# An SSM block with its gradients on one core: base powers fetched at other ticks, products with C moved, some work handed to ScalarE

## The chip, the core and the metric

One Trainium2 chip, one core of it, one launch. The metric is the device time of one execution in microseconds (us), lower is better. The engines of the core work from queues of their own, each in the order in which the program lists its instructions: PE (matrix products and transposes), VectorE (DVE), ScalarE (ACT), GpSimd (POOL), and SP, which here issues nearly all DMAs. They wait for each other through semaphores.

## The reference, cut to what matters

```python
def _A_ref(u, A_re, A_im, B_re, B_im, C_re, C_im, log_dt, Dskip):
    dt = jnp.exp(log_dt)[:, None]
    logdA = dt * (A_re + 1j * A_im)
    dB = dt * (B_re + 1j * B_im)
    P = jnp.exp(logdA[:, :, None] * l[None, None, :])         # l = 0 .. 2047
    K = jnp.einsum("dn,dnl,dn->dl", Cc, P, dB).real
    ...                                                        # y = irfft(rfft(u) * rfft(K)), the causal convolution
    return y + u * Dskip
x = A_u
xn = _layernorm(x)
s = _A_ref(xn, ...)
g = silu(einsum("bsf,fd->bsd", silu(einsum("bsd,df->bsf", xn, w1)), w2))
out = x + s * g
```

The result is `out` and the gradients of all its inputs for a given `grad_out`. L = 2048 rows, D = 512 channels, N = 128 states, F = 1792; all tensors are bf16.

## The kernel before, in words

Five stages follow each other. Stage 1 (to about 205 us of the profile) holds nearly all of the change. It does four things at once:

- `Setup`: loads x in four groups of four row tiles, takes mean and variance of each tile (`stats(i)`), normalizes it (`norm(i)`: `nb` = -mean * rstd, then `xn`), and brings the parameters A, B, C into the layout needed (`param(i)`: PE transposes into `pt_par`, a copy to `pa_...`). `lam` is eight ScalarE exponentials.
- `gen_ffn_fwd`: the forward feed-forward. Its 28 blocks (four groups of rows with seven pairs of column tiles each) give on PE a `ps_h`, from which ScalarE makes `aT` (silu) and `hs` (a copy that is stored to `hTd`). PE transposes `aT` into `pt_a`, VectorE copies that into `ak`, which is stored to `akd`. One row group later `gen_o` makes `ps_o` from `aT`; ScalarE makes `g2` (silu) and `o2` from it, which are stored to `gd` and `od`, and VectorE multiplies `g2` with `grad_out`, loaded into `G2`. "Block k" or aT(k) below counts the 28 blocks from 0.
- `dft_table_phases`: tables of sines and cosines: `tb_r`, `tb_v` on VectorE, `tb_w`, `tb_f` on ScalarE, `ps_m` and `pt_ti` on PE, stored to `TFd` and `TId`. Its first instruction is GpSimd's iota `kv`, from which VectorE casts `kf`. Its pool is opened where the pool of `Setup` (with `x_sb`) has been closed.
- `power_phases`: the base powers of exp(dt A), in eleven pairs of exponents. For pair i: `X` multiplies magnitudes on GpSimd (`ex`), `A` takes fractions of angles on VectorE (`b_r`, `b_f`), `B` takes sines on ScalarE (`b_w`, `b_s`), `C` multiplies both on VectorE into the result buffer `XYg` (two buffers), `S` stores it to `XYd` in DRAM. `setup0` makes the angle per step (`tau`), `setup1` the product of C with dt B (`Ctr`, `nCti`, twice 128x512) and the block `one`, which takes a buffer of the tag of `XYg` too. Pairs 5 and 6 (exponents 32 to 128) use `Ctr` and `nCti`.

The order is written out by hand: `stage_1` first runs six blocks with `Setup` beside them, then counts a tick n from 6 on, one block (or later half a tile of `gen_o`) per tick; what a tick starts is listed by `put`. Copies and stores handed to `later` are emitted at the end of the tick.

```python
    put(6, s0); put(8, s1); put(9, pS, "one")
    for i in range(len(PAIRS)):
        x = 7 + 2 * i + i // 5
        put(x - 1, pX, i); put(x, pA, i); put(x + 1, pB, i); put(x + 2, pC, i); put(x + 3, pS, i)
```

So the last pair (1024 and 2048) is stored at tick 32 and the one before it (768 and 896) at tick 29. At tick 30 the base powers of the first quarter of the channels are read back from `XYd` into `XYc`, in three slices, which lies in a buffer of `aT`. From tick 33 on, `copy_tables` spreads `XYc` into `X`, `Y` and `CY` on ScalarE, and `chunk_tables` multiplies out the remaining powers on VectorE (`m`). The two entries of the last pair come as a fourth fetch, `XYl`, in stage 2, where the first Fourier products (`ps_f`, `XU`) run as well. `Dskip` is loaded in `Setup` into `Dsk` and added to row 0 of the convolution kernel `K_b` at the end of stage 2.

A DMA that SP is to issue waits in SP's queue for what it needs, and with it all that stands behind it.

Of the kernel before, what the change touches and what calls it, by code (L numbers as in the profile page):

```python
# [14 lines left out]
P = 128  # L15
# [252 lines left out]
class Setup:  # L268


    def __init__(self, k, W1, W2, pr, p1):
        nc, const = k.nc, k.const
        self.k, self.pr, self.p1 = k, pr, p1
        self.names = ("A_re", "A_im", "B_re", "B_im", "C_re", "C_im")
        x_sb = self.x_sb = p1.tile([P, T, D], BF16, name="x_sb")
        nat = self.nat = p1.tile([P, 6, DK, P], BF16, name="nat")
        ldt = self.ldt = p1.tile([P, D], BF16, name="ldt")
        k.Dsk = const.tile([1, D], BF16, name="Dsk_b")
        w1v = k.ins["w1"].rearrange("(k p) f -> p k f", p=P)
# [12 lines left out]
        lx(0); ln(0)  # L292
        dma(ldt[:], k.ins["log_dt"].unsqueeze(0).to_broadcast([P, D]))
        lw(0); lx(1); lw(1); ln(1); lx(2); lw(2); lx(3); lw(3); ln(2, 3, 4, 5)
        dma(k.Dsk[:], k.ins["Dskip"].unsqueeze(0))
        dma(W2[:], k.ins["w2"].rearrange("(k p) d -> p k d", p=P))
        k.ident = make_identity(nc, const)
        li = p1.tile([P, T], I32, name="li")
        nc.gpsimd.iota(li[:], pattern=[[1, T]], base=0, channel_multiplier=T)
        mhalf = self.mhalf = p1.tile([P, T], F32, name="mhalf")  # L300
        nc.gpsimd.memset(mhalf[:], -0.5)
        k.halfpi = const.tile([P, 1], F32, name="halfpi")
        nc.vector.memset(k.halfpi[:], math.pi / 2)
# [19 lines left out]
    def norm(self, i):  # L323
        nc, k = self.k.nc, self.k
        s = slice(4 * i, 4 * i + 4)
        nc.vector.scalar_tensor_tensor(out=self.nb[:, s], in0=self.mv[:, s, 0], scalar=-1.0, in1=k.rstd[:, s], op0=ALU.mult, op1=ALU.mult)
        for t in range(4 * i, 4 * i + 4):
            nc.vector.tensor_scalar(out=k.xn[:, t, :], in0=self.x_sb[:, t, :], scalar1=k.rstd[:, t:t + 1], scalar2=self.nb[:, t:t + 1],
                                    op0=ALU.mult, op1=ALU.add)

    def param(self, i):
        nc, k = self.k.nc, self.k
        nm = self.names[i]
        pt = k.ps.tile([P, DK, P], BF16, name="pt_par", tag="ps")
        for dk in range(DK):
            nc.tensor.transpose(out=pt[:, dk, :], in_=self.nat[:, i, dk, :], identity=k.ident[:])
        t = self.pr.tile([P, D], BF16, name="pa_" + nm)
        nc.vector.tensor_copy(out=t[:], in_=pt[:].rearrange("p a b -> p (a b)"))
        k.par[nm] = t[:]

    def lam(self):
# [63 lines left out]
def power_phases(k, pr, bs, par):  # L405
# [19 lines left out]
        for x in SEU:  # L425
            nc.vector.tensor_copy(out=pv(tau, x), in_=perm(t1[:, 1], x))

    def setup1():
        dB = W2_("prt", "f", 2)
        TT(out=dB[:, 0], in0=k.dtb[:], in1=g("B_re"), op=ALU.mult)  # L430
        TT(out=dB[:, 1], in0=k.dtb[:], in1=g("B_im"), op=ALU.mult)
        for o, ba, bb in ((Ctr, 0, 1), (nCti, 1, 0)):
            t = W2_("prt", "s", 2)
            nc.vector.scalar_tensor_tensor(out=t[:, 0], in0=g("C_re"), scalar=1.0 - 2.0 * ba, in1=dB[:, ba], op0=ALU.mult, op1=ALU.mult)
            TT(out=t[:, 1], in0=g("C_im"), in1=dB[:, bb], op=ALU.mult)
            for x in SEU:
                TT(out=pv(o, x), in0=perm(t[:, 0], x), in1=perm(t[:, 1], x), op=ALU.subtract)
        one = bs.tile([P, 2, NB, 2, 64, 2], BF16, name="one", tag="XYg", bufs=2)
        nc.gpsimd.memset(one[:, 0, :, 0], 1.0); nc.gpsimd.memset(one[:, 0, :, 1], 0.0)
        for c, t in enumerate((Ctr, nCti)):  # L440
            nc.gpsimd.tensor_copy(out=part(one[:, 1:2], c), in_=by_blk(t[:].unsqueeze(1)))
        st["one"] = [(0, one[:, 0]), (20, one[:, 0]), (24, one[:, 1])]
# [31 lines left out]
    def C(i):  # L474
# [11 lines left out]
        if nc_:  # L486
# [5 lines left out]
                TT(out=c2[:, 0:nc_], in0=s[:, 0:nc_], in1=bc((nCti[:], Ctr[:])[c]), op=ALU.mult)  # L492
                TT(out=part(oc[:, 0:nc_], c), in0=by_blk(c1[:, 0:nc_]), in1=by_blk(c2[:, 0:nc_]), op=(ALU.add, ALU.subtract)[c])
            st[i] += [(25 + CEXP.index(PAIRS[i][j]), oc[:, j]) for j in range(nc_)]
    return setup0, setup1, X, A, B, C, S


def gen_ffn_fwd(k, fs, W1, W2):
# [14 lines left out]
    def trans(tc_, aT, f0):  # L513
        pt = k.ps.tile([P, 2, 4, P], BF16, name="pt_a", tag="ps")
        for j in range(2):
            for t in range(4):
                nc.tensor.transpose(out=pt[:, j, t, :], in_=aT[:, f0 + j, t * P:(t + 1) * P], identity=k.ident[:])
        ak = fs.tile([P, 2, 4, P], BF16, name="ak", tag="ak", bufs=3)
        later(k, nc.vector.tensor_copy, out=ak[:], in_=pt[:])
        later(k, nc.sync.dma_start, k.akd[f0:f0 + 2, :, 4 * tc_:4 * tc_ + 4].rearrange("f p t q -> p f t q"), ak[:])  # L520

    def gen_o(tc_, aT):
        for th in range(2):
            ts_ = slice(4 * tc_ + 2 * th, 4 * tc_ + 2 * th + 2)
            g2 = fs.tile([P, 2, D], BF16, name="g2", tag="g2", bufs=1)
            o2 = fs.tile([P, 2, D], BF16, name="o2", tag="o2", bufs=1)
            G2 = fs.tile([P, 2, D], BF16, name="G2", tag="G2", bufs=1)
            nc.sync.dma_start(G2[:], k.g_v[:, ts_, :])
            for t in range(2):
# [12 lines left out]
            later(k, later, k, nc.vector.tensor_tensor, out=k.DS[:, ts_, :], in0=G2[:], in1=g2[:], op=ALU.mult)  # L542
            yield
# [49 lines left out]
def stage_1(k):  # L593
# [24 lines left out]
    lo.close("p1")  # L618
    tab = lo.open("tab"); bs = lo.open("bs")
    tA, tB, tM, tC, tS = dft_table_phases(k, tab)  # L620
    s0, s1, pX, pA, pB, pC, pS = power_phases(k, pr, bs, k.par)
    at, mid, ready = {}, {}, []

    def put(tick, fn, *a):
# [9 lines left out]
    for x, t in sorted(ready):  # L634
        free = max(free + 1, x)
        mid.setdefault(free, []).append((tC, (t,)))
        put(free + 1, tS, t)
    put(6, s0); put(8, s1); put(9, pS, "one")
    for i in range(len(PAIRS)):
        x = 7 + 2 * i + i // 5  # L640
        put(x - 1, pX, i); put(x, pA, i); put(x + 1, pB, i); put(x + 2, pC, i); put(x + 3, pS, i)
# [8 lines left out]
    while True:  # L650
# [2 lines left out]
            fn(*a)  # L653
        if n == 28:
            k.TFs = ld_tf(k, 0)
        if n == 30:
            XY = fs.tile([P, NT, 2, 64, 2], BF16, name="XYc", tag="aT")
            for sl in (slice(0, 9), slice(9, 15), slice(17, NT)):
                nc.sync.dma_start(XY[:, sl], k.XYd[:, sl, 0])
        if n == last + 1:  # L660
            lo.close("bs", "tab", "pr")
            tables_open(k, XY)
        if n > last + 1:
# [235 lines left out]
def stage_2(k):  # L899
# [16 lines left out]
    for b in range(2):  # L916
        fr = front(b)
        if b == 0:
            last = uw.tile([P, 2, 2, 64, 2], BF16, name="XYl", bufs=1)
            nc.sync.dma_start(last[:], k.XYd[:, 15:17, 0])  # L920
            ld_tab(k, 1)
        for n, _ in enumerate(fr):
            if b == 0 and n == 0:
                nc.scalar.copy(out=cq(k.tabs[0]["X"], slice(32, 41, 8)), in_=last[:].rearrange("p i c q e -> p (c q) i e"))
            tables_0(k)
    for b in range(NB):
        Kg = chunk_K(k, b, k.tabs[b])
# [35 lines left out]
    k.do = lo.open("do")  # L963
    K_b = k.do.tile([P, T, D], BF16, name="K_b", tag="DO")
    load_K(k, K_b)
    k.masks = gen_masks(k, uw)
    next(k.masks)
    for g in (next(sl) for _ in range(4)):
        next(g)
    next(k.masks)  # L970
    nc.vector.tensor_tensor(out=K_b[0:1, 0, :], in0=K_b[0:1, 0, :], in1=k.Dsk[:], op=ALU.add)
    ro.close("uw", "cyb")
    return K_b, sl

# [818 lines left out]
```

## Time and profile before

| | us |
|---|---|
| runs of the kernel, median of 3 | 874.69 (873.41 to 877.84) |
| the profiled execution | 874.37 |
| its span in the profile | 872.6 |
| mean granted clock of TensorE | 0.892 |
| PE busy | 676.4 (78%) |
| VectorE busy | 632.0 (72%) |
| ScalarE busy | 450.6 (52%) |
| GpSimd busy | 47.6 (5%) |

Times in the text are us from the start of the span. A line of a timeline gives the start, the busy time, engine, line of the kernel, operation, what it writes and reads with its shape, and in brackets how long the engine stood idle before it and whose end released it. Several instructions of a kind are drawn together (x4). A line of the chain gives start, length and what the end of the program followed from at that time. The duration of one instruction includes a part that overlaps with the next one; the distance of two starts is the price of one in a row.

### The profile page before, as it was taken

What the parts mean: (1) busy time and instruction counts of PE and PEld (TensorE: products, weight loads), DVE (VectorE), ACT (ScalarE), POOL (GpSimd) and SP (SyncE); (2) the same over time, 40 slices, a digit from 0 to 9 for tenths busy, and PEclk for the clock granted to TensorE, in tenths of its full rate; (3) what the DMA queues carried; (4) which work ended last, traced back from release to release, by engine and by line L of the source; (5) the groups of instructions that cost most, each with busy time, mean ns of one, the idle gap of its engine ahead of it and who ended that gap; (6) DMA issues with size and microseconds to landing.
All of it is one profiled execution on the core that took longest, in us unless ns stands there. A gap on an engine that the chain in (4) does not pass through costs nothing.

```text
span 872.6 us, 13569 instructions
## 1 busy us (share of the span) xinstructions
PE 676.4 (78%) x5213; PEld 346.3 (40%) x5284; DVE 632.0 (72%) x1005; ACT 450.6 (52%) x547; POOL 47.6 (5%) x49
## 2 busy tenths in 40 slices
PE   5677886957557739766879399598688699999966
PEld 2334443423445536322334144243233355555433
DVE  6898888757999962997988999266264347776850
ACT  4459999854879835342444022054244376664231
POOL 1254221000000000000000001000000000000000
PEclk9988997987868859998989799799898899999988
DMA  9547767777769677784788685999879595668362
GB/s 273 175 149 242 266 223 257 264 250 211 217 221 305 187 195 251 266 337 148 259 333 279 209 330 209 253 250 248 208 187 205 146 224 165 177 187 277 98 202 67
DMA packets 183952, 195.18 MB, mean 224 GB/s; under 512 B 35659, under 2 KB 147791, under 8 KB 178767
## 3 DMA queue, kind: packets, MB, share of 16 engines
q1 hardware_dynamic: 179310, 185.53, 69.6%
q10 hardware_dynamic: 4577, 8.77, 3.4%
q8 instruction: 41, 0.67, 0.3%
q14 instruction: 24, 0.20, 0.1%
HBM read 110.10 MB, written 80.50 MB: 218 GB/s over the span
## 4 chain that ended last, share of the span: by engine, by line
PE 36%; DVE 28%; DMA 16%; ACT 9%; issue 6%; SPq 3%; POOL 0%; ACTq 0%; DVEq 0%; POOLq 0%
PE ps_v L1038 7%; DMA XTl<-XTd 5%; PE ps_da L1626 5%; PE ps_dx L1665 4%; PE ps_f L1014 4%; PE ps_w L1744 2%; PE ps_h L557 2%; DMA AW<-akd 2%; PE ps_w L1381 2%; DMA out_dram<-o10b 2%; DVE cm_t L106 2%; PE ps_o L533 1%; PE pt_dh L1648 1%; DVE m L747 1%; PE ps_f L894 1%
## 5 line engine op out<-in xcount | busy, mean ns | idle before, releaser
L1038 PEld LDWEIGHTS <-TIs 128*128 128x128 bf16 x384 | 39.7, 104 | 85.0 <-issue 37.8
L557 PE MATMUL ps_h<-XNT,W 128*128 128x512 bf16 x212 | 61.1, 432 | 14.7 <-ACT hs L560 13.7
L1744 PE MATMUL ps_w<-dhc,xn 128*128 128x448 bf16 x256 | 53.5, 371 | 6.9 <-ACT o10b L1746 6.9
L1531 DVE TENSOR_TENSOR T<-Vb,YTl 128x2048 bf16<-128x2048 bf16 x16 | 19.6, 1225 | 53.5 <-ACT Vb L1522 53.4
L1627 DVE TENSOR_TENSOR dhT<-ps_da,sd 128x1024 bf16<-128x1024 f32 x28 | 34.2, 1224 | 32.7 <-ACT sd L133 19.3
L1014 PEld LDWEIGHTS <-TFs 128*128 128x128 bf16 x336 | 32.9, 100 | 62.0 <-DMA TFs<-TFd 15.4
L1626 PE MATMUL ps_da<-DOT,W2T 128*128 128x512 bf16 x218 | 53.3, 384 | 2.3 <-ACT DOT L1606 1.9
L533 PE MATMUL ps_o<-W,aT 128*128 128x512 bf16 x221 | 53.1, 386 | 0.2
L1381 PE MATMUL ps_w<-DO_all,AW 128*128 128x512 bf16 x212 | 51.5, 388 | 1.9 <-issue 1.8
L1665 PE MATMUL ps_dx<-W1T,dhT 128*128 128x512 bf16 x215 | 52.0, 379 | 0.4
L855 ACT COPY XT<-pt_xt 128x1024 bf16<-128x1024 bf16 (+1 forms) x44 | 41.2, 1010 | 21.5 <-DMA K_b<-Kud 10.1
L1014 PE MATMUL ps_f<-DS,TFs 128*128 128x512 bf16 x173 | 43.3, 400 | 11.2 <-DMA TFs<-TFd 9.5
L894 PE MATMUL ps_f<-xn,TFs 128*128 128x512 bf16 x120 | 36.5, 456 | 16.9 <-ACT XU L895 15.8
L853 PE MATMUL pt_xt<-ident_bfloat,X 128*128 128x128 bf16 x328 | 29.9, 251 | 23.0 <-ACT XT L855 13.4
L1522 ACT CAST Vb<-ps_V 128x1024 bf16<-128x1024 f32 x32 | 31.7, 1013 | 28.9 <-PE ps_V L1520 21.8
L1038 PE MATMUL ps_v<-BG,TIs 128*128 128x512 bf16 x123 | 34.5, 436 | 11.9 <-DMA TIs<-TId 9.4
L1014 PE MATMUL ps_f<-K_b,TFs 128*128 128x512 bf16 x156 | 36.5, 379 | 8.8 <-ACT Ak L1016 5.1
L1038 PE MATMUL ps_v<-BK,TIs 128*128 128x512 bf16 x126 | 31.5, 404 | 13.6 <-DVE BK L97 13.5
L1744 PEld LDWEIGHTS <-xn 128*128 128x128 bf16 x256 | 26.1, 102 | 37.6 <-issue 11.1
L557 PEld LDWEIGHTS <-W 128*128 128x128 bf16 x224 | 23.3, 108 | 41.0 <-issue 25.4
L853 PEld LDWEIGHTS <-X 128*128 128x128 bf16 x328 | 25.3, 114 | 27.2 <-issue 25.4
L452 POOL TENSOR_TENSOR ex<-ex 128x512 f32<-128x512 f32 x21 | 33.0, 1582 | 53.1 <-DVE XYg L480 28.1
(287 smaller groups left out, 1457.9 us busy)
## 6 DMA issues: line engine op xcount, KB each, us to landing
TFs<-TFd SPq DMA_DIRECT2D x12, 1024.0 KB
TIs<-TId SPq DMA_DIRECT2D x24, 512.0 KB
XTd<-XT SPq DMA_DIRECT2D x20, 512.0 KB
XTl<-XTd SPq DMA_DIRECT2D x16, 640.0 KB
UXl<-UXd SPq DMA_DIRECT2D x8, 1024.0 KB
hTd<-hs SPq DMA_DIRECT2D x28, 256.0 KB
akd<-ak SPq DMA_DIRECT2D x28, 256.0 KB
AW<-akd ACTq DMA_DIRECT2D x14, 512.0 KB
```

The costliest lines, as they stand in the source:

```text
L533: nc.tensor.matmul(out=pso[:], lhsT=aT[:, ft, tt * P:(tt + 1) * P], rhs=W2[:, ft, :], start=(ft == 0), stop=(ft == FT - 1))
L557: nc.tensor.matmul(out=ps[:, j], lhsT=W1[:, dk, ft * P:(ft + 1) * P], rhs=XNT[:, dk], start=(dk == 0), stop=(dk == DK - 1))
L853: nc.tensor.transpose(out=pt[:, j, c], in_=X[:, c, P * kk:P * kk + P], identity=k.ident[:])
L855: nc.scalar.copy(out=XT[:, j0:j0 + len(ks)], in_=pt[:, 0:len(ks)])
L894: nc.tensor.matmul(out=ps[:, c, :], lhsT=TFs[:, t1 + 4 * j, c, :], rhs=src[:, t1 + 4 * j, :], start=(j == 0), stop=(j == 3))
L1014: nc.tensor.matmul(out=ps[:, c, :], lhsT=tab(j), rhs=src[:, t1 + 4 * j, :], start=(n == 0), stop=(n == 4 * len(terms) - 1))
L1038: nc.tensor.matmul(out=ps[:, j, :], lhsT=TIs[:, j, 2 * kt + c, :], rhs=B[kt][:, c, (t0 + j) % 4, :], start=(kt == 0 and c == 0), stop=(kt ...
L1381: nc.tensor.matmul(out=ps[:], lhsT=A[:, t, :], rhs=k.DO[:, t, :], start=(t == 0), stop=(t == T - 1))
L1626: nc.tensor.matmul(out=ps[:, j], lhsT=self.W2T[:, dk, ft * P:(ft + 1) * P], rhs=self.DOT[tc_][:, dk], start=(dk == 0), stop=(dk == DK - 1))
L1627: nc.vector.tensor_tensor(out=self.dhT[:, f0:f0 + 2, :], in0=ps[:], in1=sd[:], op=ALU.mult)
L1665: nc.tensor.matmul(out=psx[:], lhsT=dhT[:, ft, t % 4 * P:(t % 4 + 1) * P], rhs=self.W1T[:, ft, :], start=(ft == 0), stop=(ft == FT - 1))
L1744: nc.tensor.matmul(out=ps[:], lhsT=k.xn[:, t, dk * P:(dk + 1) * P], rhs=ch[i][:, t, :], start=(t == 0), stop=(t == T - 1))
```

## The change

- `XYc`: the slices 0 to 8 and 17 to 27 are fetched at tick 28, the slice 9 to 14 still at tick 30. `XYl` is fetched at tick 33 into a tile of the constant pool.
- `g2` gets the pool's two buffers instead of one, `ak` two instead of three.
- `setup1` is cut in two pieces, one for `Ctr` at tick 12 and one for `nCti` at tick 14, each with the products with dt made anew and in place; `setup2` with the block `one` is at tick 15, its stores at tick 16. The pieces use the tag `r` of VectorE's fractions in place of the tags `f` and `s`.
- `xn` of the tiles 3 and 8 to 15 is made by ScalarE, and so are the copies of the four parameters B and C.
- `Dskip` is loaded at the end of stage 2, behind the loads of `K_b`.

```diff
@@ Setup
-        k.Dsk = const.tile([1, D], BF16, name="Dsk_b")
+        k.XYl = const.tile([P, 2, 2, 64, 2], BF16, name="XYl")
...
-        dma(k.Dsk[:], k.ins["Dskip"].unsqueeze(0))
@@ norm
-            nc.vector.tensor_scalar(out=k.xn[:, t, :], in0=self.x_sb[:, t, :], scalar1=k.rstd[:, t:t + 1], scalar2=self.nb[:, t:t + 1],
-                                    op0=ALU.mult, op1=ALU.add)
+            if i >= 2 or t == 3:
+                nc.scalar.activation(out=k.xn[:, t, :], in_=self.x_sb[:, t, :], func=ACT.Identity, scale=k.rstd[:, t:t + 1], bias=self.nb[:, t:t + 1])
+            else:
+                nc.vector.tensor_scalar(out=k.xn[:, t, :], in0=self.x_sb[:, t, :], scalar1=k.rstd[:, t:t + 1], scalar2=self.nb[:, t:t + 1],
+                                        op0=ALU.mult, op1=ALU.add)
@@ param
-        nc.vector.tensor_copy(out=t[:], in_=pt[:].rearrange("p a b -> p (a b)"))
+        (nc.scalar.copy if i > 1 else nc.vector.tensor_copy)(out=t[:], in_=pt[:].rearrange("p a b -> p (a b)"))
@@ power_phases
-    def setup1():
-        dB = W2_("prt", "f", 2)
-        TT(out=dB[:, 0], in0=k.dtb[:], in1=g("B_re"), op=ALU.mult)
-        TT(out=dB[:, 1], in0=k.dtb[:], in1=g("B_im"), op=ALU.mult)
-        for o, ba, bb in ((Ctr, 0, 1), (nCti, 1, 0)):
-            t = W2_("prt", "s", 2)
-            nc.vector.scalar_tensor_tensor(out=t[:, 0], in0=g("C_re"), scalar=1.0 - 2.0 * ba, in1=dB[:, ba], op0=ALU.mult, op1=ALU.mult)
-            TT(out=t[:, 1], in0=g("C_im"), in1=dB[:, bb], op=ALU.mult)
-            for x in SEU:
-                TT(out=pv(o, x), in0=perm(t[:, 0], x), in1=perm(t[:, 1], x), op=ALU.subtract)
+    def setup1(i):
+        dB = W2_("prt", "r", 1)
+        TT(out=dB[:, 0], in0=k.dtb[:], in1=g("B_re" if i == 0 else "B_im"), op=ALU.mult)
+        TT(out=dB[:, 1], in0=k.dtb[:], in1=g("B_im" if i == 0 else "B_re"), op=ALU.mult)
+        nc.vector.scalar_tensor_tensor(out=dB[:, 0], in0=g("C_re"), scalar=1.0 - 2.0 * i, in1=dB[:, 0], op0=ALU.mult, op1=ALU.mult)
+        TT(out=dB[:, 1], in0=g("C_im"), in1=dB[:, 1], op=ALU.mult)
+        for x in SEU:
+            TT(out=pv((Ctr, nCti)[i], x), in0=perm(dB[:, 0], x), in1=perm(dB[:, 1], x), op=ALU.subtract)
+
+    def setup2():
         one = bs.tile([P, 2, NB, 2, 64, 2], BF16, name="one", tag="XYg", bufs=2)
@@ gen_ffn_fwd
-        ak = fs.tile([P, 2, 4, P], BF16, name="ak", tag="ak", bufs=3)
+        ak = fs.tile([P, 2, 4, P], BF16, name="ak", tag="ak")
...
-            g2 = fs.tile([P, 2, D], BF16, name="g2", tag="g2", bufs=1)
+            g2 = fs.tile([P, 2, D], BF16, name="g2", tag="g2")
@@ stage_1
-    put(6, s0); put(8, s1); put(9, pS, "one")
+    put(6, s0); put(12, s1, 0); put(14, s1, 1); put(15, s2); put(16, pS, "one")
...
+        if n == 28:
+            XY = fs.tile([P, NT, 2, 64, 2], BF16, name="XYc", tag="aT")
+            for sl in (slice(0, 9), slice(17, NT)):
+                nc.sync.dma_start(XY[:, sl], k.XYd[:, sl, 0])
         if n == 30:
-            XY = fs.tile([P, NT, 2, 64, 2], BF16, name="XYc", tag="aT")
-            for sl in (slice(0, 9), slice(9, 15), slice(17, NT)):
-                nc.sync.dma_start(XY[:, sl], k.XYd[:, sl, 0])
+            nc.sync.dma_start(XY[:, 9:15], k.XYd[:, 9:15, 0])
         if n == last + 1:
+            nc.sync.dma_start(k.XYl[:], k.XYd[:, 15:17, 0])
             lo.close("bs", "tab", "pr")
@@ stage_2
-            last = uw.tile([P, 2, 2, 64, 2], BF16, name="XYl", bufs=1)
-            nc.sync.dma_start(last[:], k.XYd[:, 15:17, 0])
...
+    Dsk = uw.tile([1, D], BF16, name="Dsk_b", bufs=1)
+    nc.sync.dma_start(Dsk[:], k.ins["Dskip"].unsqueeze(0))
```

More of the change, by code (lines that the diff above doesn't have):

```diff
@@ L494, in C @@
             st[i] += [(25 + CEXP.index(PAIRS[i][j]), oc[:, j]) for j in range(nc_)]
-    return setup0, setup1, X, A, B, C, S
+    return setup0, setup1, setup2, X, A, B, C, S
 def gen_ffn_fwd(k, fs, W1, W2):
@@ L620, in stage_1 @@
     tA, tB, tM, tC, tS = dft_table_phases(k, tab)
-    s0, s1, pX, pA, pB, pC, pS = power_phases(k, pr, bs, k.par)
+    s0, s1, s2, pX, pA, pB, pC, pS = power_phases(k, pr, bs, k.par)
     at, mid, ready = {}, {}, []
@@ L923, in stage_2 @@
             if b == 0 and n == 0:
-                nc.scalar.copy(out=cq(k.tabs[0]["X"], slice(32, 41, 8)), in_=last[:].rearrange("p i c q e -> p (c q) i e"))
+                nc.scalar.copy(out=cq(k.tabs[0]["X"], slice(32, 41, 8)), in_=k.XYl[:].rearrange("p i c q e -> p (c q) i e"))
             tables_0(k)
@@ L970, in stage_2 @@
     next(k.masks)
-    nc.vector.tensor_tensor(out=K_b[0:1, 0, :], in0=K_b[0:1, 0, :], in1=k.Dsk[:], op=ALU.add)
+    nc.vector.tensor_tensor(out=K_b[0:1, 0, :], in0=K_b[0:1, 0, :], in1=Dsk[:], op=ALU.add)
     ro.close("uw", "cyb")
```

## The prediction

> **What bounds the kernel now.** I read the busy time by stage first, because the change touches only the first 205 us and one 1 KB load at 324 us. Columns: stage, its length, then PE, PEld, DVE (VectorE), ACT (ScalarE), POOL (GpSimd) busy us.
>
> ```profile
> 22.00:44.00 22.00, 14.72 (x106) 8.33 (x106) 19.20 (x51) 10.98 (x14) 5.81 (x9) 0.92 0.50 174
> 44.00:66.00 22.00, 15.47 (x95) 8.23 (x95) 21.65 (x40) 12.86 (x16) 12.64 (x8) 0.84 0.43 146
> 66.00:128.00 62.00, 53.88 (x364) 29.33 (x371) 53.52 (x60) 60.88 (x78) 18.79 (x13) 0.94 0.72 246
> 177.00:205.00 28.00, 12.93 (x52) 5.40 (x52) 13.63 (x26) 13.47 (x18) 0.00 (x0) 0.81 0.84 257
> ```
>
> Three stages, three limits. From 22 to 66 us VectorE sets the pace (21.65 of 22 us). From 66 to 128 ScalarE does (60.88 of 62), with VectorE close behind. From 177 to 205 no engine is half busy: that stage waits. Second, the chain that ended last (start, us, what) and SP's waits say for what:
>
> ```profile
> 176.81 8.21 DMA XYc<-XYd
> 185.12 2.30 ACT X L720 x2
> ...
> 190.69 0.61 ACT g L76
> 191.30 0.57 ACT o L76
> ...
> 197.07 6.87 DMA XYl<-XYd
> ...
> 203.96 0.69 ACT X L924
> ```
>
> ```profile
> SPq L659 <- DMA XYd<-XYg: 5.4, 1, 5.4
> ```
>
> Two fetches of the base powers stand on the path. In the first, the middle slice waits 5.4 us in SP's queue for the store of powers 768 and 896. Third, the timelines of VectorE and ScalarE (start, duration, what, idle before):
>
> ```profile
> 26.60 1.38 DVE L328 TENSOR_SCALAR xn<-x_sb,rstd,nb 128x512 bf16<-128x512 bf16 x4
> 28.50 0.41 DVE L338 COPY pa_B_re<-pt_par 128x512 bf16<-128x512 bf16 x1
> 47.73 0.68 DVE L430 TENSOR_TENSOR prt<-dtb,pa_B_re 128x512 f32<-128x512 bf16 x1
> 80.81 0.69 DVE L76 COPY ak<-pt_a 128x1024 bf16<-128x1024 bf16 x1 [2.54 <-PE pt_a L517]
> 92.40 0.69 DVE L76 COPY ak<-pt_a 128x1024 bf16<-128x1024 bf16 x1 [2.12 <-PE pt_a L517]
> ```
>
> ```profile
> 43.26 0.72 ACT L378 ACTIVATE tb_f<-tb_w,halfpi 128x512 bf16<-128x512 f32 x1
> 174.66 0.60 ACT L76 ACTIVATE g<-ps_o 128x512 bf16<-128x512 f32 x1 [2.30 <-DMA gd<-g]
> ```
>
> The two idle stretches at 80.81 and 92.40 are the only large ones of VectorE between 44 and 105: the room for the moved products.
>
> **xn and four parameters to ScalarE: +3.2 us at tick 6.** Off VectorE go two groups of four xn (26.60 to 27.90, 1.3 each) and four copies (28.50 to 29.28 and 37.19 to 37.85): 4.0 us. But ScalarE takes its work in order, and each xn group is put ahead of the next block's aT, and needs nb, which VectorE has only after the statistics. The price of one: 128x512 activations without a per-partition operand start 0.53 apart (42.21, 42.74), the one with a per-partition bias takes 0.61 (43.26 to 43.87); xn has two such operands. Bounds 0.53 and 0.80, taken 0.70 (one more step of 0.09), so 2.8 a group.
> Now the places. xn 3 stands behind lam, which ScalarE ends at 11.06: done near 11.85, where VectorE had it at 10.9. The transposes and all after them start 0.95 later. ScalarE then runs out at 23.6 and stands for nb until 27.5; aT(3), which ran at 22.91, comes at 30.4. Queued behind it are hs(3), the two B copies and aT(4). PE's transposes of block 3 wait for it, and VectorE, free at 28.2, gets its ak(3) at 32.1: 3.9 idle. After the second group there is another: the first instruction of the table stage, GpSimd's iota kv, lies in x_sb's memory and has to wait for the last xn, in before until 36.07, now until 40.4; VectorE is free at 38.8 and gets kv at 41.1: 2.3. Sum: 0.95 - 4.0 + 3.9 + 2.3 = 3.2 later. With 0.53 an instruction it is about 1.8.
> The Trainium skill, "ScalarE: Activation LUTs", Rules for kernel authors, speaks against this part: add and mul belong on VectorE, up to about three times faster there in bf16. The trace's 0.33 against some 0.70 agrees. By that rule, all of the part left where it was, the sum below would be 3.2 lower.
>
> **The products with C: -6.4, then +4.9.** Out of 47.73 to 54.99 go six products (0.60 each) and sixteen small subtractions: 7.26 us, 0.9 of them stretched by GpSimd's casts beside them, so 6.4 off a stage where VectorE has no idle. ScalarE's 4.7 us wait at 51.84 (b_s needed their buffers) goes too. So VectorE's b_f for the second pair, due 64.24, comes 3.2 earlier net, and ScalarE, which waits for it (4.15 us at 64.34), starts its full stretch 3.2 earlier.
> Back they come in two pieces at ticks 12 and 14, now eight products (dB is computed twice): 2.4 + 1.6 = 4.0 each. If they land in the two idle stretches, 4.0 - 2.54 + 4.0 - 2.12 = 3.4 is left on the path, since b_f of ticks 13 and 15 is used at once: ScalarE took them 0.1 us after (88.52) and after 0.83 us of waiting (100.73). GpSimd is the second cost: its queue has the casts of Ctr and nCti ahead of the powers of pair 5, so two multiplies that ran at 71.6 run near 95. A DVE fraction beside GpSimd takes 1.42 where it takes 0.69 alone; 0.7 a multiply makes 1.5 (0 to 3.3 with the casts). The block "one" now uses the result buffer just ahead of pair 4: its three stores are issued at tick 16, some 102.9 in before, and land about 4.2 later, after pair 4's product (103.86) wants the buffer. That is 3.2 us, behind which ak and the next fractions queue; VectorE's idle at 107.16 (0.73) and 116.36 (2.29) takes it up. I take 0, at most 3.2.
>
> **Fetches: -3.1.** XYl is issued at tick 33 rather than behind the 1 MB TFs load of stage 2, so its 6.87 us leave the chain. VectorE's step at 204.68 can follow the one that ends at 199.35: 5.3 saved. Whoever queues behind the waiting XYl on SP (the last gd and od, at 195.68) comes later anyway.
> The two early slices cost some of it. They put 1,280 KB ahead of the store that the middle slice waits for. 576 KB of such 512-byte pieces landed in 2.5 us (182.6 to 185.12), so this is 5.5 us on a queue that was full. The store is then seen at about 188, and the middle slice, gd and od go out behind it. od matters: o2 keeps a single buffer, and ScalarE's o at 191.30 needs it. With an empty queue after 188, od lands near 193.4, so the middle copy starts 2.2 later; the first copies start at 181 instead of 185, which nobody needs. Bounds 0 (od no later than now) and 5.3 (the whole gain). -5.3 + 2.2 = -3.1.
> The Trainium skill, "DMA: Bandwidth & Descriptors", Specifications, has 512 bytes as enough for line rate, at about 358 GB/s per core from HBM. By it, 1.31 MB would take 3.7 us (an estimate), 1.8 less, and the sum would be that much lower. The row says 230 KB per us, and I keep it.
>
> **Edits at nothing.** g in two buffers: the 2.30 at 174.66 is only g's. The o behind it needs od, issued 0.98 after gd, so ScalarE stands there until about the same 175.2; 0 taken, 2.3 saved if od lands early. ak in two buffers instead of three: the store two blocks back is mostly long landed; in the crowded first 30 us it may cost 0.6, which lies inside the 3.9 above. Dskip: one more 1 KB issue on SP after K_b's loads (0.40 us); the add that needs it ran at 319.2, while VectorE's next work is at 332.15 and PE's first use at 331.95. Without that cover it would cost some 2.5.
>
> **The sum.** Profiled execution 874.4 (span 872.6 and 1.8 around it; the median of the runs is 874.7). 3.2 - 6.4 + 3.4 + 1.5 - 3.1 = -1.4: **873.0 us**. No stage behind 205 us hides or adds anything: VectorE is full from 205 to 250, and what starts earlier stays earlier.
>
> **Rivals.**
> Faster, the products fit: what VectorE gains by tick 11 becomes room ahead of tick 12, and xn costs 0.53. For it: GpSimd no longer runs beside VectorE at 64 to 74. Against: VectorE then waits for PE's tile, as at 80.81. 1.8 - 6.4 + 0 + 1.5 - 3.1 = -6.2: 868.2. Chance 0.20.
> Slower, VectorE becomes the bound of ticks 12 to 17: with ScalarE and PE ahead by 3 us, their tiles lie ready and the idle of 2.54 and 2.12 is gone, so all 8.0 us are on the path, and the wait for the stores of "one" too (3.2). 3.2 - 6.4 + 8.0 + 1.5 + 3.2 - 3.1 = +6.4: 880.8. For it: VectorE is within 0.1 us of ScalarE at 88.52. Against: the idle was made by PE waiting on ScalarE, which stays full. It decides from about 4 us more than I count. Chance 0.08.
> The fetch gives all back: od is late by the full 5.5 us. +1.7: 876.1. For it: SP issues od only after the middle slice. Against: the queue is empty then. Chance 0.12.
> My forecast: 0.60; its own range is 869.5 to 876.5.
>
> **From these to numbers.** Half a percent is 4.4 us, about what a measurement of this kernel can tell from no change. Faster by more (under 870.3): 0.17 of the first rival and 0.06 of the forecast's low side, 0.23. Slower by more (over 879.1): 0.06 of the second and 0.01 more, 0.07. Within: 0.70. The range 867 to 878 leaves out most of the slower rival and the lower part of the faster one.
>
> **What would show it.** In the profile after: aT(3) near 30 and kf near 41 (right), or aT(3) under 26 (the xn term is wrong); ScalarE's b_w of the second pair near 61; b_w of pair 4 within 1.5 us of 102 in place of 100.73; ScalarE without a wait for XYl, and a wait before o near 185 to 193. If o does not wait there, or the pieces find VectorE idle for their full 4 us, the kernel is faster than I say.

## The result, and the profile after

The changed kernel takes 881.56 us (median of 19 runs, 876.66 to 886.03), the kernel before on the same chip 875.62 (19 runs, 869.45 to 880.39): ratio 1.0063, 95% interval 1.0040 to 1.0086, so slower by about 5.9 us, small but clear of the interval. A second set of runs gave 1.0077 (1.0045 to 1.0110). The forecast was 873.0 with a range of 867 to 878; the measured time lies above the range. The profiled execution took 882.52 us, span 880.7.

The busy time by stage, with the columns as before the change (stage, length, PE, PEld, VectorE, ScalarE, GpSimd):

```profile
22.00:44.00 22.00, 12.44 (x97) 7.26 (x95) 12.32 (x29) 15.21 (x20) 4.69 (x7) 0.92 0.42 144
44.00:66.00 22.00, 17.21 (x116) 9.08 (x117) 21.49 (x29) 16.55 (x23) 10.48 (x9) 1.00 0.41 139
66.00:128.00 62.00, 50.55 (x351) 28.18 (x356) 54.71 (x80) 57.45 (x74) 20.48 (x14) 0.94 0.76 259
177.00:205.00 28.00, 14.95 (x67) 6.70 (x68) 15.99 (x29) 15.41 (x22) 0.00 (x0) 0.83 0.80 248
```

In the first row VectorE has lost 6.9 us of work, in the second it is as full as before, with 29 instructions in place of 40: fewer, but longer. ScalarE is no longer full from 66 to 128. Where the time went is in VectorE's timeline (start, duration, what, idle before it and who ended that):

```profile
32.75 0.69 DVE L76 COPY ak<-pt_a 128x1024 bf16<-128x1024 bf16 x1 [4.31 <-PE pt_a L519]
41.75 0.43 DVE L359 CAST kf<-kv 128x512 f32<-128x512 int32 x1 [2.01 <-POOL kv L357]
44.54 1.75 DVE L426 SCALAR_TENSOR_TENSOR prt<-dtb,pa_A_im 128x512 f32<-128x512 bf16 x1
46.33 5.98 DVE L428 COPY tau<-prt 128x64 f32<-128x64 f32 x8
...
77.39 0.68 DVE L432 TENSOR_TENSOR prt<-dtb,pa_B_re 128x512 f32<-128x512 bf16 x1
81.37 0.71 DVE L76 COPY ak<-pt_a 128x1024 bf16<-128x1024 bf16 x1
93.78 0.67 DVE L76 COPY ak<-pt_a 128x1024 bf16<-128x1024 bf16 x1
94.89 1.41 DVE L253 SCALAR_TENSOR_TENSOR tb_v<-kf,lf,tb_r 128x512 f32<-128x512 f32 x1
96.22 2.21 DVE L482 TENSOR_TENSOR XYg<-ex,b_w 128x1024 bf16<-128x1024 f32 x1
110.59 1.36 DVE L482 TENSOR_TENSOR XYg<-ex,b_w 128x1024 bf16<-128x1024 f32 x1 [3.34 <-DMA XYd<-one]
```

The first two rows are the waits that the forecast named for xn. Then tau's eight copies, which took 1.11 us in the kernel before, take 5.98. The copies of `ak` at 81.37 and 93.78 have lost their idle time, as forecast. GpSimd's timeline stands beside it:

```profile
42.98 9.01 POOL L454 TENSOR_TENSOR ex<-ex 128x512 f32<-128x512 f32 x7
83.95 2.18 POOL L443 CAST one<-Ctr 128x512 bf16<-128x512 f32 x1
93.31 1.18 POOL L443 CAST one<-nCti 128x512 bf16<-128x512 f32 x1 [7.18 <-DVE nCti L437]
94.43 10.98 POOL L454 TENSOR_TENSOR ex<-ex 128x512 f32<-128x512 f32 x6
```

The kernel before had these rows for the same work:

```profile
42.07 1.11 DVE L426 COPY tau<-prt 128x64 f32<-128x64 f32 x8
51.87 1.77 POOL L441 CAST one<-Ctr 128x512 bf16<-128x512 f32 x1 [11.77 <-DVE Ctr L437]
55.75 14.61 POOL L452 TENSOR_TENSOR ex<-ex 128x512 f32<-128x512 f32 x8
71.64 2.57 POOL L452 TENSOR_TENSOR ex<-ex 128x512 f32<-128x512 f32 x2 [1.29 <-DVE XYg L480]
```

There the casts of `one` stood behind the first multiply and held GpSimd until 55 us, long after tau was done. In the changed kernel seven multiplies run beside tau's copies. Later GpSimd stands 7.18 us for `nCti` with six multiplies queued behind (before, three pairs at 71.64, 84.75 and 96.95), which then run in one go beside the next product and fractions. ScalarE waits for what these delay (xn for `nb`, b_w of pairs 0 and 4 for VectorE), and for `od` at the end of the stage:

```profile
27.79 2.93 ACT L328 ACTIVATE xn<-x_sb,nb,rstd 128x512 bf16<-128x512 bf16 x4 [3.93 <-DVE nb L325]
55.18 1.06 ACT L467 ACTIVATE b_w<-b_f 128x1024 f32<-128x1024 f32 x1 [5.11 <-DVE b_f L253]
104.31 1.06 ACT L467 ACTIVATE b_w<-b_f 128x1024 f32<-128x1024 f32 x1 [4.17 <-DVE b_f L253]
197.56 0.58 ACT L76 CAST o<-ps_o 128x512 bf16<-128x512 f32 x1 [7.15 <-DMA od<-o]
204.21 0.74 ACT L927 COPY X<-XYl 128x512 bf16<-128x512 bf16 x1
```

The last row has no bracket: ScalarE no longer waits for XYl. The chain that ended last (start, us, what) and SP's wait show what came in its place:

```profile
187.09 5.24 DMA XYd<-XYg
192.41 0.37 SPq L663
192.88 0.49 SPq L76
193.46 4.02 DMA od<-o
197.56 0.58 ACT o L76
```

```profile
SPq L663 <- DMA XYd<-XYg: 4.7, 1, 4.7
```

The middle slice still waits for the store of powers 768 and 896, `od` goes out behind it, and `o` waits for `od`.

### The profile page after: what moved, and what is told of

It is laid out like the page before. It is cut to its first block, busy times and chain, and to the rows that moved or that the text cites. A ratio compares the mean times of both kernels' runs of the same rounds, so it can differ in the third digit from the quotient of the medians.

```text
span 880.7 us, 13573 instructions
## 1 busy us (share of the span) xinstructions
PE 673.8 (77%) x5213; PEld 344.9 (39%) x5284; DVE 629.6 (71%) x994; ACT 458.5 (52%) x560; POOL 47.8 (5%) x49
## 4 chain that ended last, share of the span: by engine, by line
DVE 32%; PE 29%; DMA 19%; ACT 8%; issue 7%; SPq 4%; POOL 0%; ACTq 0%; DVEq 0%; another core or an unknown queue 0%; POOLq 0%
PE ps_da L1631 5%; DMA XTl<-XTd 4%; PE ps_f L1019 4%; PE ps_dx L1670 4%; PE ps_v L1043 3%; PE ps_w L1386 3%; DMA AW<-akd 3%; PE ps_w L1749 2%; DVE m L752 2%; DVE m L750 2%; DVE cm_t L106 2%; DMA out_dram<-o10b 2%; PE ps_h L559 2%; DVE m L766 2%; PE pt_dh L1653 1%
## 5 line engine op out<-in xcount | busy, mean ns | idle before, releaser
L1043 PEld LDWEIGHTS <-TIs 128*128 128x128 bf16 x384 | 38.9, 103 | 82.5 <-issue 32.3
L1019 PE MATMUL ps_f<-DS,TFs 128*128 128x512 bf16 x173 | 44.5, 409 | 11.9 <-DMA TFs<-TFd 9.1
L899 PE MATMUL ps_f<-xn,TFs 128*128 128x512 bf16 x120 | 33.5, 429 | 14.2 <-ACT XU L900 13.2
L1043 PE MATMUL ps_v<-BG,TIs 128*128 128x512 bf16 x123 | 32.7, 418 | 12.3 <-DMA TIs<-TId 9.9
L1679 ACT ACTIVATE dxn<-dxn,c,rstd 128x512 f32<-128x512 f32 x16 | 13.0, 814 | 42.8 <-DVE c L1678 42.8
```

Source lines behind the costliest of these rows:

```text
L899: nc.tensor.matmul(out=ps[:, c, :], lhsT=TFs[:, t1 + 4 * j, c, :], rhs=src[:, t1 + 4 * j, :], start=(j == 0), stop=(j == 3))
L1019: nc.tensor.matmul(out=ps[:, c, :], lhsT=tab(j), rhs=src[:, t1 + 4 * j, :], start=(n == 0), stop=(n == 4 * len(terms) - 1))
L1043: nc.tensor.matmul(out=ps[:, j, :], lhsT=TIs[:, j, 2 * kt + c, :], rhs=B[kt][:, c, (t0 + j) % 4, :], start=(kt == 0 and c == 0), stop=(kt ...
```

## The experiments

Each kernel was timed against the kernel before on the same chip. I read five landmarks of the first stage in each profile: the start of ScalarE's b_w for pairs 1, 3, 4 and 10, and of VectorE's first `XU` (start of stage 2's own work). The kernel before was profiled three times and the changed one twice; the rows give the means. Three profiles of before agree to 0.2 us up to pair 4, 0.3 at pair 10 and 0.8 at `XU`. The changed kernel and skip_early, with the same first stage, spread more: 1.3 at pair 4, 1.7 at pair 10, 3.4 at `XU`. The other kernels were profiled once each. So single differences under 2 us are read with care, and the readings below rest as far as possible on steps between landmarks that several kernels share.

| kernel | pair 1 | pair 3 | pair 4 | pair 10 | XU | ratio (95%) |
|---|---|---|---|---|---|---|
| before | 64.4 | 88.5 | 100.7 | 176.0 | 221.4 | 1 |
| changed | 64.3 | 88.6 | 104.4 | 181.9 | 223.7 | 1.0063, 1.0077 |
| xn_only | 68.1 | 92.5 | 104.7 | 180.9 | 224.6 | 1.0062 (1.0033 to 1.0092) |
| split_only | 60.7 | 85.8 | 101.6 | 179.5 | 225.0 | 1.0029 (0.9998 to 1.0060) |
| split_tau | 58.2 | 82.4 | 98.2 | 175.0 | 219.9 | 0.9997 (0.9972 to 1.0023) |
| split_late | 60.5 | 85.4 | 97.4 | 174.1 | 219.0 | 0.9976 (0.9956 to 0.9997) |
| xyl_only | 63.0 | 87.1 | 99.3 | 174.4 | 214.5 | 0.9950 (0.9927 to 0.9974) |
| fetch_all | 64.3 | 88.4 | 100.5 | 176.1 | 218.1 | 0.9960 (0.9939 to 0.9982) |
| skip_late | 63.3 | 87.6 | 99.7 | 175.0 | 220.2 | 1.0016 (0.9988 to 1.0045) |
| skip_early | 64.6 | 89.8 | 105.6 | 183.3 | 226.1 | 1.0037 (1.0014 to 1.0060) |
| mended | 62.5 | 87.3 | 99.3 | 176.3 | 219.0 | 0.9982 (0.9955 to 1.0008) |
| combined | 58.2 | 82.5 | 94.4 | 171.2 | 211.2 | 0.9889 (0.9861 to 0.9917) |
| combined_par | 56.4 | 80.8 | 92.7 | 169.7 | 209.9 | 0.9891 (0.9860 to 0.9922) |

**xn_only.** The kernel before with the two edits in `norm` and `param` alone.

```diff
+            if i >= 2 or t == 3:
+                nc.scalar.activation(out=k.xn[:, t, :], ..., func=ACT.Identity, scale=k.rstd[:, t:t + 1], bias=self.nb[:, t:t + 1])
...
+        (nc.scalar.copy if i > 1 else nc.vector.tensor_copy)(out=t[:], ...)
```

> The kernel before plus one part: seven or nine normalisations (t = 3 and t = 8 to 15) and four parameter copies run on ScalarE. Theory 'pays at the start and is carried': aT(3) comes 3.9 us later less 4.0 us off VectorE as in the changed kernel, kf 3.2 to 3.9 us later, and the end 3 to 4 us later: 879. Rival 'absorbed': before, VectorE waits for GpSimd's products and ScalarE for VectorE in the ticks behind, so the lag at 45 us is gone by 100 us: 875.6 within 1. Rival 'gains': tau's copies run before GpSimd's multiplies and VectorE is free earlier: 872.

Measured 881.74 us, ratio 1.0062. The lag is 3.6 us at pair 1, 4.0 at pair 4 and 3.2 at `XU`: it is carried to the end. This part alone loses as much as the whole change.

**split_only.** The kernel before with `setup1` in two pieces at ticks 12 and 14, `one` at 15, its stores at 16.

```diff
-    put(6, s0); put(8, s1); put(9, pS, "one")
+    put(6, s0); put(12, s1, 0); put(14, s1, 1); put(15, s2); put(16, pS, "one")
```

> The kernel before plus one part: C's products are made at ticks 12 and 14 in two pieces, the casts of 'one' follow at 15, its stores at 16. Theory 'contention': GpSimd's first seven multiplies now start near 43 us beside tau's eight copies (1.11 us before, 5.98 us in the changed kernel), which gives back 5 of the 6.4 us that leave VectorE; the second piece and the six GpSimd multiplies near 94 us cost 3 to 4 more: 877 to 879, and tau's copies take over 4 us. Rival 'the normalisations were to blame': without them GpSimd's multiplies meet no copies, tau stays near 1.1 us, b_w of pair 1 comes near 58 us and the whole gains 3 us: 872.5.

Measured 879.27 us, ratio 1.0029. Tau's copies take 4.02 us here although xn stays on VectorE, so the rival falls. It is 3.7 us ahead at pair 1, 0.9 behind at pair 4, 3.5 behind at pair 10.

**split_tau.** split_only plus one element copied by GpSimd ahead of its multiplies, so that they start behind tau.

```diff
     def X(i):
         t = W2_("ex", "ex", 4)
+        if i == 0:
+            nc.gpsimd.tensor_copy(out=k.tw[:], in_=tau[:, D - 1:D])
```

> split_only (the kernel before with C's products in two pieces at ticks 12 and 14) plus a one-element copy on GpSimd that reads the last element of tau before GpSimd's first multiply, so that the seven multiplies start only when tau's eight copies are done. Theory 'contention': tau's copies take 1.1 us again (4.02 us in split_only, 1.11 before), the sums ahead of them (L424 1.76 us, L253 1.41) go back to about 0.7, b_w of pair 0 starts 4 to 5 us earlier than in split_only (46 to 47), and what GpSimd does later costs VectorE less, since then it runs f32 multiplies and not small copies; the median falls by 2 to 4 us against split_only's 879.3, to 875 to 877. Rival 'only shifted': the slow-down is paid by whichever VectorE instruction stands beside GpSimd's multiplies; b_w of pair 1 comes as in split_only (60.7) and the median stays at 879.

Measured 876.8 us, ratio 0.9997 against split_only's 1.0029. Its groups of VectorE between 38 and 46 us (line, operation, shape, count, then busy us and mean ns of one):

```profile
L253 DVE SCALAR_TENSOR_TENSOR b_f<-tau,b_r 128x512 f32<-128x512 f32 x2 | 2.8, 1408 | 0.1
L252 DVE TENSOR_SCALAR b_r<-tau 128x512 int32<-128x512 f32 x2 | 1.9, 972 | 0.0
L427 DVE COPY tau<-prt 128x64 f32<-128x64 f32 x8 | 1.1, 210 | 0.0
```

In the changed kernel:

```profile
L428 DVE COPY tau<-prt 128x64 f32<-128x64 f32 x8 | 6.0, 818 | 0.0
```

The same seven multiplies, now from 42.04 us on, stand beside the fractions that follow. The two `b_f` take 1,408 ns each, 691 in the kernel before. Of the two `b_r` the first (0.56 us) starts ahead of the multiplies, the second takes 1.38 us for a usual 0.42, so the 972 is a mean of unlike rows. The table's next fraction slows as well. A slowed instruction loses 0.4 to 1.0 us, but fewer stand there than the eight copies. It is 2.5 us ahead of split_only at pair 1 and 3 to 5 later (combined against split_late: 2.3): most of "contention" is confirmed, and "only shifted" falls, though a part of the price is indeed shifted.

**split_late.** split_only with the casts of `one` at tick 18 and its stores at 19.

```diff
-    put(6, s0); put(12, s1, 0); put(14, s1, 1); put(15, s2); put(16, pS, "one")
+    put(6, s0); put(12, s1, 0); put(14, s1, 1); put(18, s2); put(19, pS, "one")
```

> split_only with the casts of 'one' at tick 18 and its stores at tick 19 (15 and 16 there). Theory 'blocked queue': in split_only GpSimd sat behind the cast of nCti until 90.6 us and then ran six multiplies in one go (91.72, 11.01 us), beside which VectorE lost some 3.6 us (b_w of pair 3 2.75 us ahead of before, of pair 4 0.9 us behind); with the casts later the multiplies come two at a time, b_w of pair 4 is again 2 to 3 us ahead of before (98), and the median falls by 3 us to 876. Rival 'second piece': the 3.6 us are the piece's own four microseconds on a VectorE without idle time; b_w of pair 4 stays near 101.6 and the median near 879. Third: the casts only move the stall to the fifth product (C of pair 5 waits for the stores of 'one'), 3 us later: 879 with b_w of pair 6 late.

Measured 875.03 us, ratio 0.9976. GpSimd no longer stands in the way at 90 us (its timeline), and VectorE's second piece with what follows runs at its usual pace (its timeline):

```profile
66.23 2.57 POOL L452 TENSOR_TENSOR ex<-ex 128x512 f32<-128x512 f32 x2 [6.82 <-DVE XYg L480]
102.95 0.99 POOL L439 MEMSET one<- 128x512 bf16 x2 [34.16 <-DMA XYd<-XYg]
```

```profile
86.10 0.68 DVE L430 TENSOR_TENSOR prt<-dtb,pa_B_im 128x512 f32<-128x512 bf16 x1
88.63 1.57 DVE L435 TENSOR_TENSOR nCti<-prt 128x64 f32<-128x64 f32 x8
91.83 0.75 DVE L253 SCALAR_TENSOR_TENSOR tb_v<-kf,lf,tb_r 128x512 f32<-128x512 f32 x1
92.50 1.37 DVE L480 TENSOR_TENSOR XYg<-ex,b_w 128x1024 bf16<-128x1024 f32 x1
```

The fraction that took 1.41 us and the product that took 2.21 in the changed kernel take 0.75 and 1.37. In all five VectorE instructions stand beside the six multiplies there, from the fraction at 94.89 to the one at 102.86: they take 7.8 us together, 3.9 at their usual pace. From pair 3 to pair 4 before takes 12.2 us. The kernels with the casts at tick 15 (changed twice, skip_early, split_only, split_tau) take 15.7 to 15.9, those with the casts at tick 18 (split_late, mended, combined, combined_par) 11.9 to 12.0. So the piece's own 4 us cost nothing there, and the rival "second piece" falls. GpSimd did not run two multiplies at a time, as I had put it; it stood idle for 34 us waiting for the buffer of `one`, and its six multiplies came at 105.5 us for 8.40 us, where 1.3 us are lost by pair 6. The third reading falls as well: between 100 and 130 us VectorE does not wait for the stores of `one`.

**xyl_only and fetch_all.** The kernel before with XYl at tick 33 in a tile of its own and Dskip loaded at 205 us; fetch_all has XYc's outer slices at tick 28 and two buffers for g and ak as well.

```diff
         if n == last + 1:
+            nc.sync.dma_start(k.XYl[:], k.XYd[:, 15:17, 0])
```

> The kernel before plus one part: XYl is loaded in the first stage into memory of its own (Dskip's place is taken, Dskip is loaded at 205 us into uw). XYc stays at tick 30, g single, xn on VectorE, C's products in one piece. Theory 'the fetch alone is good': the 5.3 us wait of ScalarE for XYl at 205 us goes and nothing else is paid: 870.3 of 875.6. Rival 'hidden anyway': VectorE's chain of table copies sets the time at 220 us, not the copy of XYl; within 1 us of 875.6. Rival 'pushed': the load sits on SP ahead of XTd and the first loads of the second stage; 877 to 878.

> The kernel before with the whole of the fetch part (XYc's first two slices at tick 28, the middle one at 30, XYl early into its own memory, g in two buffers, ak in two) and Dskip loaded at 205 us. Theory 'the wait only moved from g to o': xyl_only's 871.8 within 1.5 us, since in the changed kernel g waited 1.86 us and o 1.50 us, and the first copy of X came only as early as the load of its last slice. Rival 'two steps sooner pays': 869 to 870, two microseconds better than xyl_only. Rival 'the early loads push the stores of od': o (the second pair) waits over 5 us on od and the time is 874 or more.

Measured 871.8 us (0.9950) and 873.72 us (0.9960). ScalarE's waits between 165 and 215 us, in us in total, times, and the longest, first of xyl_only, then of fetch_all:

```profile
ACT X L720 <- DMA XYc<-XYd: 5.4, 1, 5.4
ACT g L76 <- DMA gd<-g: 4.9, 2, 2.6
```

```profile
ACT o L76 <- DMA od<-o: 8.6, 2, 7.6
ACT X L722 <- DMA XYc<-XYd: 2.6, 1, 2.6
```

From pair 10 to `XU` before takes 45.4 us, xyl_only 40.1 (combined and combined_par 40.0 and 40.2), fetch_all 42.0 (the others with its fetches 41.1 to 42.8). XYl alone is worth 5.3 us; the two steps sooner, with g and ak in two buffers, give 1.9 of it back, on `od`. Which of these edits gives it back was not tried apart. The medians of the two do not tell them apart, the profiles do. In fetch_all `o` waited 7.6 us on `od`, as the last rival said, but the time stayed under its 874. Ahead of pair 1, xyl_only differs from before only by the missing load of Dskip and is 1.4 us ahead there; skip_late, which lacks it too, is 1.1 ahead, fetch_all 0.1. So no effect of that load is shown.

**skip_early and skip_late.** The changed kernel with Dskip loaded when `uw` opens, and the kernel before with Dskip loaded behind K_b.

```diff
@@ stage_2, behind uw = ro.open("uw", 2)
+    Dsk = uw.tile([1, D], BF16, name="Dsk_b", bufs=1)
+    nc.sync.dma_start(Dsk[:], k.ins["Dskip"].unsqueeze(0))
```

> The changed kernel with one thing undone in effect: the load of Dskip (1 KB) is issued when the pool uw opens (near 205 us) and no longer behind the twenty-odd loads of K_b. Theory 'Dskip': in the changed kernel the add on K_b ran at 333.88 us after 13.95 us of idle time on VectorE (319.20 us and no wait before), and ps_f came 2.4 us later than before; with the early load the add runs near 320 us, ps_f starts within 0.5 us of the end of ps_dsk, and the median falls by 2.4 us against the changed kernel's 881.6, to 879.2, half of the loss. Rival 'carried in from the first stage': the wait only ate slack, the time stays within 1 us of 881.6. Rival 'all of it': 875.6, as before, because everything behind 330 us hangs on that point.

> The kernel before with one thing changed: Dskip is loaded behind the loads of K_b into uw, as in the changed kernel. Theory 'Dskip': the add on K_b waits near 14 us for it (13.95 in the changed kernel) and ends about 1.8 us after ps_dsk would have let ps_f start; ps_f, and everything to 540 us, comes 1.8 to 2.4 us later, and the median is 2 us over before, ratio 1.002. Rival 'absorbed': the stages behind 540 us wait for transfers anyway, ratio 1.000 within its interval though the traces differ at 335 us.

Measured 880.03 us (1.0037) and 877.96 us (1.0016). In skip_late the timelines of VectorE and PE show the wait, and that PE had to stand for it:

```profile
330.42 0.41 DVE L971 TENSOR_TENSOR K_b<-K_b,Dsk_b 1x512 bf16<-1x512 bf16 x1 [12.96 <-DMA Dsk_b<-in_A_Dskip_dram]
330.88 3.61 PE L1014 MATMUL ps_f<-K_b,TFs 128*128 128x512 bf16 x15 [1.79 <-DVE K_b L971]
```

PE waits 1.79 us here, 0.91 and 1.03 in the two profiles of the changed kernel, and not at all in skip_early. Most of VectorE's 13 us is slack. By these waits of PE the price is 1 to 2 us, under the 2.4 that I had read from the first pair of profiles. Neither median resolves it.

**mended.** The changed kernel with three mends: GpSimd waits for tau, `one` at ticks 18 and 19, Dskip at 205 us.

> The changed kernel with three mends: GpSimd's multiplies wait for tau, the casts of 'one' come at tick 18 and its stores at 19, Dskip is loaded at 205 us. xn and four parameters stay on ScalarE, XYc at tick 28, g in two buffers. Theory 'the parts add up': combined (0.989) plus the price of xn_only (0.006) plus fetch_all against xyl_only (0.001): ratio 0.996, some 873; b_w of pair 1 near 62 (58.2 in combined plus 3.7), tau near 1.1 us. Rival 'xn was only bad together with the contention': ratio 0.989 to 0.991, b_w of pair 1 under 60. Rival 'the products come too late': with kf at 41.7 us and the wait for tau GpSimd's first products miss C of pair 0 and the ratio is 1.000 or more.

Measured 875.19 us, ratio 0.9982; its interval holds the 0.996 of "the parts add up" and not the 0.989 of the first rival. It reaches 1.0008, so the median alone does not exclude the second rival; the profile does: pair 1 comes at 62.5 (near 62 was expected), and VectorE does not wait for GpSimd's products before it. With xn's lag left in, the rest of the change gains about what xn costs.

**combined and combined_par.** xyl_only plus the split with its two mends; combined_par puts the four parameter copies on ScalarE too. xn stays on VectorE, g single, XYc at tick 30.

> xyl_only plus the split with both mends (GpSimd waits for tau; casts of 'one' at tick 18, stores at 19); xn on VectorE, g single, XYc at tick 30. Theory 'contention and blocked queue': the split keeps the 3.6 us that it was ahead at 60 to 75 us in split_only (b_w of pair 1 60.70 for 64.34), so 868 (871.8 less 3.6). Rival 'no slack on VectorE': the pieces cost their 4 us each wherever they stand and the end of the first stage comes when xyl_only's does: 872. Rival 'a new stall by the stores of one': 874 or more.

> combined (867.4) plus four parameter copies on ScalarE, the normalisations staying on VectorE. Theory 'only the normalisations cost': four copies of 0.41 us leave VectorE ahead of kf (37.6 us), ScalarE has idle time there (5.53 us ahead of 40.3), so tau comes 0.8 to 1.6 us earlier and the median is 866. Rival 'ScalarE pays': they stand in ScalarE's queue ahead of aT and hs, the chain of hidden columns waits, and the median is 868 to 870.

Measured 867.43 us (0.9889, interval 0.9861 to 0.9917) and 865.78 us (0.9891, 0.9860 to 0.9922): both are faster than the two kernels of the case, combined by 9.7 us of 877.7. It is 10.2 us ahead at `XU`. The parameter copies bring 1.3 us more at `XU`, which the medians do not resolve; nothing speaks for "ScalarE pays".

**after_again, before_again and before_third.** The two kernels of the case, unchanged.

> The changed kernel once more, unchanged, for a second profile. Theory 'the first stage repeats, the last ones do not': the landmarks up to 100 us (tau's copies, b_w of pairs 0 to 4) come within 1 us of the first profile (46.3, 55.2, 64.8, 75.8, 88.6, 104.3), the first XU between 222.7 (the first profile) and 226.1 (skip_early, whose first stage is the same), K_b's add waits near 14 us again; behind 540 us differences of 2 to 3 us are of the execution. Rival: the first profile was a good example of all, and everything lies within 1 us to the end.

> The kernel before, unchanged, for a second profile. Theory 'a quick example': from the first store of dKgd to the end it takes 333.5 to 337 us, as in the other kernels, and the first stage comes as in the first profile to within 1 us (b_w of pair 4 at 100.7, XYl's copy at 204). Rival 'the change slows the end too': 330 us again, so that 4 us or more of the loss arise behind 540 us by something that every edit here touches.

> The kernel before, unchanged, for a third profile; as for before_again: 333.5 to 337 us behind the first store of dKgd if the first profile was a quick example, 330 if the stretch belongs to the kernel.

The first stage repeats: tau's copies take 5.99 us again, pairs 0 to 2 come 1.0 us sooner, pair 4 at 104.4 (104.3). The end does not. From the first store of `dKgd` to the end (counted, as in the expectations, from some 2.3 us after SP issues it at about 540 us), the first profile of before took 330.0 us, the other two 333.6 and 335.1, the changed kernel 335.9 and 336.0, and the other kernels up to then 333.5 to 339.1. The first profile of before was a quick example there, so the 8.1 us between the first two spans overstate the change. By the means of all profiles the changed kernel is 2.3 us behind at `XU`, 3.8 at 540 us and 6.9 at the end. Whether the last 3 us belong to the change is open: the stretch varies by more than that between executions of like kernels.

## Why the prediction was wrong, step by step

**The step that failed.** It is the cost of GpSimd in the move of the products. The forecast had one pair of multiplies run late, beside VectorE's fractions, for +1.5 us, and +3.4 for the pieces themselves, so the move was to bring -6.4 + 3.4 + 1.5 = -1.5 us. What the runs showed in its place: GpSimd cost 2.5 us beside tau's copies and 3.6 between pairs 3 and 4, the pieces nothing, so that by pair 4 the move brought -6.2 + 2.5 + 3.6 = -0.1. Beside that, three terms were too small: xn, the stretch around the stores of `one`, and Dskip.

**xn on ScalarE, +3.2.** Right in mechanism. One xn started 0.71 us after the other (2.83 from the first to the aT behind four; 0.70 was taken), aT(3) came at 30.62 (30.4), kf at 41.75 (41). In xn_only the lag is 3.6 us at pair 1, 5.0 at pair 10, 3.2 at `XU`, and the median says 5.4 (1.0062 of 876.7). The rule weighed there, of the Trainium skill ("ScalarE: Activation LUTs", Rules for kernel authors), that add and mul belong on VectorE, is borne out for xn by this loss of 0.6%. It names no copies, and the four copies cost nothing here (combined_par against combined).

**Products with C, -6.4 off the early stage.** The forecast had pair 1 near 61; it came at 64.8 and 63.8. The work did leave, and with GpSimd held behind tau (split_tau) pair 1 is 6.2 us ahead of before. What failed is the claim that GpSimd's moved multiplies are those at 71.6 that would run near 95. I followed the multiplies behind the casts' new place, not those ahead of it: with the casts gone from GpSimd's queue at 39 us, seven multiplies came forward to 43 us and met tau's copies. The term "+1.5 (0 to 3.3)" named the right resource at the wrong place. It measures 2.5 us at pair 1, by split_only against split_tau. With xn's 3.6 and the 6.2, the changed kernel's 0 at pair 1 is the sum: 3.6 - 6.2 + 2.5 = -0.1. The shares depend on the order in which the parts are added: from combined over mended to the changed kernel, the same 6.1 us are 4.3 for xn with the four copies and 1.8 for GpSimd beside tau.

**Two pieces, +3.4.** The size from pair 3 to pair 4 was right by luck (3.6 us, 100.7 to 104.4 while pair 3 is unmoved), the cause wrong. The first piece cost nothing (pair 3 as far ahead as pair 1 in split_tau), nor did the second (split_late). A price of 0 for the pieces is the term of the rival "Faster, the products fit" (chance 0.20), which in this was right. The 3.6 us are the six multiplies that queued behind the cast of `nCti`, where the forecast had two, and ran beside a product of pair 3 and pair 4's fractions.

**The wait for the stores of "one", 0, at most 3.2.** Pair 4's product waited 3.34 us for it in the profile (110.59). From pair 4 to pair 6 the lag grows by 1.2 and 2.1 us in the changed kernel, 1.3 in split_late and 2.2 in split_only; GpSimd's multiplies stand in the same stretch. In split_late VectorE has no such wait and the 1.3 us are lost all the same, so the wait itself may cost nothing to 1 us; the two are not separated further. For the stretch the value 0 was too low, and the bound of 3.2 holds.

**Fetches, -3.1.** Right, term by term: -5.3 for XYl (xyl_only), +1.9 for `od` (2.2 was taken), and the wait ahead of `o` that the forecast named, 7.15 us until 197.56. From pair 10 to `XU` the changed kernel takes 41.1 and 42.6 us against 45.4.

**Dskip at nothing.** The cover named, to 331.95 for PE's ps_f and 332.15 for VectorE, was too short: it leaves 6 us after the issue at 325.5, and the 1 KB needed 8.3 (the chain has 325.51 to 333.77). The forecast had not asked how long the load would take behind K_b's loads. It cost 1 to 2 us; for the 2.5 that the forecast put without cover it gives no row.

**"No stage behind 205 us hides or adds anything."** What a kernel leads or lags at `XU` it has within 2.7 us in its median too, the changed kernel within 4.4; so it holds roughly, without Dskip and the 3 us that stay open.

**The sum.** So of the 7.3 us between -1.4 and +5.9, some 4 arise before pair 10 (+1.7 without the fetches was forecast, 5.9 measured): up to 2 on xn, 1 at tau, 1 to 2 around `one`. 1 to 2 are Dskip, and the rest is open. The rival "VectorE becomes the bound" gave 880.8, near the time measured, by luck: its mechanism, pieces without idle time to land in, is not what happened: split_late has them in the same place for nothing.

**The price of standing beside GpSimd.** Eight copies of 64 elements took 818 ns each beside GpSimd's multiplies and 208 without, and a multiply takes some 1.3 us (9.01 for seven): a copy loses about half of one. An instruction three times as long loses little more: 0.72 us for a `b_f` of 0.69. The Trainium skill, "SBUF — State Buffer", section "Who interferes with whom", says that VectorE and GpSimd share a pair of ports under an exclusive lock held for a whole instruction, and that copies in the two-port modes contend for it, and instructions with two SBUF inputs where GpSimd's instruction reads SBUF. The trace agrees for the fractions with two inputs (`b_f`, `tb_v`) and the products; in which mode tau's copies ran no run shows. So in these rows the price goes by the number of VectorE instructions beside GpSimd more than by their length.

## What to carry to other kernels

When work moves from one place to another, list what stood behind it in every queue and now comes forward, before pricing where it lands: here the harm came from GpSimd multiplies that no edit names. Put a train of GpSimd instructions beside few long VectorE instructions rather than beside a row of short ones; a one-element copy is enough to hold it back. A part that only removes a wait (XYl) is worth trying apart from its neighbours: alone it gained 0.5%, and with the split and its two mends 1.1%, where the bundle lost 0.6%.

## What the runs showed of the hardware

- A 128x64 f32 copy of VectorE takes 208 ns alone (before) and 818 ns in the mean beside GpSimd's f32 multiplies (the changed kernel). Fractions of 128x512 go from 0.69 to 1.41 us (`b_f`) and from 0.42 to 1.38 (`b_r`), in split_tau. VectorE's copies of 128x1024 from `pt_a` do not slow down: 0.68 us at 64.24 and 67.09 in the kernel before, beside its eight multiplies.
- A 1 KB load issued behind 2 MB of K_b's loads landed after 8.3 us (the changed kernel, 325.51 to 333.77).
- PE's pace after a long wait differs between executions of one kernel. Near 560 us PE stands 9.4 to 10.1 us for a load, runs sixteen products, and behind a second wait of 1.3 to 2.8 us come eight of `ps_w`. Those eight take 1.90 us in the first and third profile of before and in the second of the changed kernel, but 3.55 and 3.59 in before_again and the first of the changed kernel. In that last one the granted clock was 0.58 from 571 to 579 us, in the first profile of before 1.00 from 567 to 575. What decides it is not shown; it is a part of what makes the end vary.
